# Pooled attention with a gated MLP on one core: batch 0's query loads on ScalarE's queue, w_in's v-half in four loads, the left-over sums apart, and a new opening order

## The chip, the cores and the metric

The kernel runs on one core of a Trainium2 chip. The core has five engines with an instruction stream each: TensorE (PE in the profile), VectorE (DVE), ScalarE (ACT), GpSimd (POOL) and SyncE (SP), which here only issues loads and stores. The metric is device time in microseconds (us), the median over executions; lower is better.

## What is computed

For 8 batches, 8 heads, 576 positions and 64 numbers per head, keys and values are averaged over groups of 8 positions, so 72 of each are left. All 576 queries attend to the 72 pooled keys. The result, 576 x 512 per batch, is the input x of a gated MLP whose output is added to x.

```python
k_p = k.reshape(B, H, Sp, 8, D).mean(axis=3)
v_p = v.reshape(B, H, Sp, 8, D).mean(axis=3)
scores = scale * np.matmul(q, k_p.transpose(0, 1, 3, 2))
attn = np.exp(scores - scores.max(-1)) ; attn = attn / (attn.sum(-1) + 1e-09)
x = np.matmul(attn, v_p)                       # then to (B, S, H*D)
h = gelu_tanh(x @ w_in)                        # 512 -> 1024
u, v = h[..., :512], h[..., 512:]
v_n = (v - mean(v)) / sqrt(var(v) + 1e-06) * g_ln
v_s = einsum('ts,bsd->btd', w_sg, v_n) + b_sg[None, :, None]
out = x + (u * v_s) @ w_out
```

All inputs are float32 but w_in and w_out, which come as float64 and are read as pairs of 32-bit integers.

## The kernel before

The work is cut into steps with a letter, a number and a batch. For a batch: A and B load pooled groups of keys and values (two loads each, per group of four heads), E loads what is left over of the 72 rows after 64 ("left"), C loads the queries of two heads. K sums groups of eight keys; P does so for values. Q turns the queries (into `qT`), S forms the scores of two heads and runs the softmax, T and L turn the probabilities, V multiplies them with the values and writes x, split into two addends (`xhl`) so that the products stay exact. H is the v-half of `x @ w_in` for 128 positions with gelu and normalization, U the u-half, W the product with `w_sg`, O the product with `w_out`, Z the store. A lower-case letter is a weight: `lv0` loads a part of the v-half of w_in, `v0` to `v3` convert and split its quarters, likewise `lu`, `u` for the u-half, `lo`, `o` for w_out, `ls`, `s` for w_sg.

A list, PROLOGUE, gives the order of all these pieces up to the steady state, and PERIOD the order of one batch after that; each mention of a name runs its step up to the next `yield`. Every engine takes its instructions strictly in the order in which they were recorded (the dependencies that the last lines of the function add see to that). So the two lists fix what stands behind what on each engine, and the only freedom at run time is when each waits.

In batch 0, keys and values are summed by TensorE, with a matrix `apart` that picks rows (`pool8`); the left-overs of keys and values lie in one tile, 32 partitions each, and one VectorE instruction sums both (`psum8(lp[64:P], ...)`). ScalarE copies the sums out of PSUM (`kp`), TensorE turns them, ScalarE writes them into `kbd`, and S multiplies `kbd` with `qT`. In later batches VectorE makes the sums.

PSUM is used as two rings of two tiles, `mps` and `aps`; SWAP names the steps that take a tile of the other ring. A tile is taken again only when its last reader is done.

All loads go through SP's queue. A DMA signals one of eight semaphores, taken in turn; a load waits until the one eight before it has landed, so at most eight are under way. The first half of w_in's v-half is one load of 1 MB (`lv0`, 128 x 2 x 1024 integers), the second another (`lv1`). The queries of batch 0 are loaded as they lie in memory (NATURAL), 96 x 6 x 64 numbers for each head: two loads for each of four pairs of heads, the first three pairs into a tile called `early`, the fourth into `qraw`. `early` also holds batch 0's values.

Of the kernel before, what the change touches and what calls it, by code (L numbers as in the profile page):

```python
# [20 lines left out]


PROLOGUE = """
A1+0 A0+0 lv0 E0+0 K0+0 v0 C0+0 C1+0 C2+0 K0+0 C3+0 K1+0 K2+0 K1+0 K2+0 Q0+0 Q1+0 v0 v0 v1 ls0 K2+0 v1 Q0+0 S0+0 Q2+0
Q1+0 S0+0 v1 S1+0 S0+0 B1+0 lv1 S0+0 S1+0 Q2+0 v1 S0+0 S2+0 S1+0 S0+0 S0+0 S2+0 v1 S1+0 v0 S0+0 v0 S2+0 Q3+0 B0+0
Q3+0 S1+0 S3+0 S2+0 S1+0 T0+0 A1+1 S2+0 s3 S1+0 E0+1 S0+0 s4 T0+0 S3+0 S3+0 S3+0 S2+0 S2+0 S1+0 s3 s4 S3+0 s3 S2+0
S3+0 lu0 S3+0 S2+0 s2 s4 P1+0 S3+0 s2 P0+0 v2 A0+1 s2 C0+1 S1+0 S3+0 C1+1 T1+0 v3 L0+0 T2+0 v3 P2+0 L0+0 T1+0 V0+0
lo0 v2 T2+0 V0+0 T3+0 V1+0 v2 v2 s1 v3 K2+1 T3+0 K1+1 K0+1 v3 V1+0 V3+0 v2 V0+0 s1 K2+1 Q0+1 V2+0 s1 v3 B0+1 u0 u0
K2+1 Q1+1 V3+0 V2+0 V1+0 S0+1 S1+1 S0+1 V3+0 u1 V2+0 S0+1 H0+0 H2+0 S1+1 lu1 u0 S0+1 S1+1 V3+0 V2+0 S0+1 S1+1 u1 S0+1
u1 S0+1 H0+0 H0+0 H2+0 C2+1 s0 u1 u0 S1+1 u1 V1+0 H0+0 H3+0 C3+1 s0 V0+0 U1+0 u0 P0+1 S1+1 H2+0 u3 s0 u3 u2 H2+0 u2  # L30
U1+0 H4+0 H0+0 H4+0 Q2+1 T0+1 S1+1 Q3+1 S2+1 T0+1 H2+0 u2 B1+1 S0+1 u3 u2 H4+0 H0+0 H1+0 H2+0 H4+0 T0+1 S2+1 S2+1 u2
H4+0 H3+0 u3 u3 P1+1 H1+0 H3+0 S3+1 S1+1 S3+1 S2+1 S3+1 P2+1 lb0 S2+1 H3+0 U2+0 H1+0 U0+0 o1 S3+1 C0+2 S2+1 U2+0 H4+0
S3+1 H3+0 S3+1 H4+0 S2+1 S3+1 C1+2 A0+2 U3+0 H1+0 U0+0 H3+0 P2+1 S2+1 H4+0 S3+1 K0+2 P2+1 o1 T1+1 H1+0 lo1 A1+2 U3+0
L0+1 P2+1 L0+1 H1+0 L0+1 o0 W2+0 V0+1 o1 L0+1 o0 T1+1 W3+0 T1+1 B0+2 o0 E0+2 o1 o0 V1+1 Q0+2 o1 V0+1 W2+0 K1+2 o3 o3
T2+1 T2+1 o0 T2+1 W3+0 V1+1 W0+0 V2+1 Q1+2 o2 T3+1 o2 T3+1 W0+0 o3 B1+2 W1+0 o2 W3+0 K2+2 T3+1 W1+0 V1+1 K2+2 V2+1
W0+0 V3+1 W3+0 K2+2 S0+2 S1+2 W0+0 C2+2 W2+0 C3+2 W1+0 V3+1 P1+2 W1+0 W2+0 S0+2 O0+0 S1+2 o2 O0+0 Q2+2 S0+2 O1+0 O0+0
o2 V0+1 S1+2 S0+2 o3 o3 P0+2 V2+1 O1+0 A0+3 A1+3 S2+2 V3+1 O2+0 P2+2 S1+2 S2+2 S2+2 V1+1 O1+0 C0+3 O2+0 S0+2 O2+0
H2+1 V3+1 Z0+0 T0+2 Z0+0 H2+1 Q3+2 Z1+0
""".split()
# [776 lines left out]
```

## Time and profile before

| | |
|---|---|
| median of 3 runs | 573.52 us (573.29 to 575.09) |
| the profiled run | 575.11 us, span 573.3 us, granted clock 0.997 |
| TensorE busy | 552.2 us, 96% of the span |
| VectorE | 408.8 us, 71% |
| ScalarE | 345.9 us, 60% |
| GpSimd | 229.8 us, 40% |
| moved by DMA | 46.34 MB |

A busy share over the whole span is a mean over an opening, seven periods of 66 us in which TensorE works without a pause, and an end. In the views, a row of the timeline gives start, length, engine, line, operation, tiles (written<-read), count, and in brackets how long the engine had stood idle ahead of it and what ended that. L166 is the one line from which all loads are issued and L111 the one from which nearly all products are, so there the tiles tell the steps apart: `mps<-xhl,wih` 128x288 is U, `mps<-wih,xhl` 128x512 is H, `aps<-kbd,qT` is S, `ident,e` is T, `ident,el` is L.

### The profile page before, as it was taken

What the parts mean: (1) busy time and instruction counts of PE and PEld (TensorE: products, weight loads), DVE (VectorE), ACT (ScalarE), POOL (GpSimd) and SP (SyncE); (2) the same over time, 40 slices, a digit from 0 to 9 for tenths busy, and PEclk for the clock granted to TensorE, in tenths of its full rate; (3) what the DMA queues carried; (4) which work ended last, traced back from release to release, by engine and by line L of the source; (5) the groups of instructions that cost most, each with busy time, mean ns of one, the idle gap of its engine ahead of it and who ended that gap; (6) DMA issues with size and microseconds to landing.
All of it is one profiled execution on the core that took longest, in us unless ns stands there. A gap on an engine that the chain in (4) does not pass through costs nothing.

```text
span 573.3 us, 10301 instructions
## 1 busy us (share of the span) xinstructions
PE 552.2 (96%) x3793; PEld 520.9 (91%) x3793; DVE 408.8 (71%) x570; ACT 345.9 (60%) x947; POOL 229.8 (40%) x310
## 2 busy tenths in 40 slices
PE   3799999999999999999999999999999999999996
PEld 3677799998999999998999989999999989998996
DVE  1889999888568775878667785778667765344454
ACT  1588695977558755677647766497546775412320
POOL 3477765753144341713325331523416131433240
PEclk9899999999999999999999999999999999999999
DMA  7996545164413435152421625132440211021105
GB/s 196 312 244 164 107 144 116 20 136 78 97 24 74 82 71 105 38 104 62 96 34 44 115 57 106 51 77 46 96 79 1 43 21 22 1 42 22 21 1 84
DMA packets 161602, 46.34 MB, mean 81 GB/s; under 512 B 149072, under 2 KB 149072, under 8 KB 161552
## 3 DMA queue, kind: packets, MB, share of 16 engines
q1 hardware_dynamic: 156688, 45.10, 36.4%
q10 hardware_dynamic: 4864, 0.59, 0.7%
q8 instruction: 30, 0.49, 0.4%
q14 instruction: 20, 0.16, 0.1%
HBM read 36.23 MB, written 9.44 MB: 80 GB/s over the span
## 4 chain that ended last, share of the span: by engine, by line
PE 85%; DMA 5%; DVE 4%; ACT 2%; SPq 2%; issue 1%; POOL 0%; DVEq 0%; ACTq 0%
PE mps L111 68%; PE aps L111 13%; PE aps L146 3%; SPq L166 2%; DMA raw<-in_moe_w_in 2%; DMA kvraw<-in_k 1%; DMA stage<-in_moe_w_sg 1%; DVE kp L335 1%; DMA qraw<-in_q 1%; ACT lt L506 0%; DVE vp L335 0%; DVE lp L335 0%; ACT vl L414 0%; DVE e L485 0%; DVE e L460 0%
## 5 line engine op out<-in xcount | busy, mean ns | idle before, releaser
L111 PE MATMUL mps<-xhl,wih 128*128 128x288 f32 x512 | 89.8, 297 | 0.0
L111 PE MATMUL mps<-wih,xhl 128*128 128x512 f32 x248 | 83.0, 401 | 0.1
L111 PEld LDWEIGHTS mps<-xhl,wih 128*128 128x128 f32 x512 | 75.8, 188 | 1.5
L687 POOL TENSOR_TENSOR glo<-u,ghi 128x576 fp32r<-128x576 f32 x28 | 40.1, 1443 | 91.8 <-ACT ghi L685 91.8
L467 ACT ACTIVATE e<-aps,nmax 128x72 f32<-128x72 f32 x240 | 73.2, 352 | 1.5 <-DVE nmax L450 1.2
L111 PE MATMUL mps<-wsh,vhh 128*128 128x288 f32 x248 | 57.1, 301 | 0.1
L467 ACT ACTIVATION_READ_ACCUMULATOR e<-aps,nmax 128x1 f32 x240 | 57.1, 239 | 0.0
L111 PEld LDWEIGHTS mps<-wih,xhl 128*128 128x128 f32 x248 | 46.6, 188 | 10.6 <-DVE x L726 0.3
L111 PE MATMUL mps<-wsh,vhl 128*128 128x288 f32 x248 | 55.7, 295 | 0.0
L111 PE MATMUL mps<-wsl,vhh 128*128 128x288 f32 x248 | 55.4, 294 | 0.0
L111 PE MATMUL mps<-xhl,wil 128*128 128x288 f32 x256 | 55.0, 296 | 0.0
L111 PE MATMUL mps<-ghi,woh 128*128 128x288 f32 x240 | 54.1, 301 | 0.4 <-DVE u L655 0.4
L557 POOL TENSOR_TENSOR xhl<-x,xhl 128x576 fp32r<-128x576 f32 x32 | 45.3, 1427 | 22.6 <-ACT xhl L555 22.6
L605 DVE TENSOR_SCALAR vg<-vg,mv,rstd 128x512 f32<-128x512 f32 (+1 forms) x40 | 40.3, 1007 | 19.4 <-POOL rstd L603 19.4
L602 POOL TENSOR_TENSOR rstd<-mv,eps 128x1 f32<-128x1 f32 (+1 forms) x40 | 10.7, 267 | 105.3 <-DVE mv L600 95.9
L111 PE MATMUL mps<-glo,woh 128*128 128x288 f32 x240 | 52.7, 295 | 0.0
L111 PE MATMUL mps<-ghi,wol 128*128 128x288 f32 x240 | 52.6, 295 | 0.0
L676 DVE SCALAR_TENSOR_TENSOR mps<-mps,gcol,bbc 128x576 f32<-128x576 f32 x27 | 22.2, 824 | 39.1 <-PE mps L111 39.1
L111 PE MATMUL mps<-wil,xhl 128*128 128x512 f32 x124 | 49.0, 395 | 0.0
L595 ACT ACTIVATE vg<-mps 128x512 f32<-128x512 f32 x31 | 18.5, 598 | 47.4 <-PE mps L111 47.2
L615 POOL TENSOR_TENSOR vhl<-vg,vhh 128x512 fp32r<-128x512 f32 x32 | 41.8, 1308 | 8.5 <-ACT vhh L613 8.5
L111 PE MATMUL aps<-kbd,qT 128*128 128x144 f32 x300 | 41.2, 288 | 2.7 <-DVE e L485 1.4
(208 smaller groups left out, 1427.1 us busy)
## 6 DMA issues: line engine op xcount, KB each, us to landing
kvraw<-in_k SPq DMA_DIRECT2D x32, 256.0 KB
qraw<-in_q SPq DMA_DIRECT2D x112, 72.0 KB
out<-y SPq DMA_DIRECT2D x112, 72.0 KB
kvraw<-in_v SPq DMA_DIRECT2D x28, 256.0 KB
raw<-in_moe_w_in SPq DMA_DIRECT2D x4, 1024.0 KB
raw<-in_moe_w_out SPq DMA_DIRECT2D x2, 1024.0 KB
stage<-in_moe_w_sg SPq DMA_DIRECT2D x4, 288.0 KB
left<-in_k SPq DMA_DIRECT2D x16, 64.0 KB
```

What stands on the lines that cost most here:

```text
L111: nc.tensor.matmul(o, lhsT, rhs, start=start, stop=stop)
L146: nc.tensor.transpose(ps[:rows, i * P:(i + 1) * P], src(i), ident if i < NT - 1 else swap)
L166: queue.dma_start(o, i)
L335: nc.vector.tensor_reduce(out=o, in_=t.rearrange("p a (r d) -> p a d r", r=POOL), axis=AX.X, op=ALU.add)
L467: nc.scalar.activation(e[:, i, h], slots[i][:, h], AF.Exp, bias=nmax[:, i, h:h + 1], **acc)
L557: (nc.vector if b in LO_DVE else nc.gpsimd).tensor_tensor(xhl[:, 1, g], x32[:, g], xhl[:, 0, g].bitcast(F32), op=ALU.subtract)
L595: nc.scalar.activation(vg, o, AF.Gelu_apprx_tanh)
L602: nc.gpsimd.tensor_tensor(rstd, mv[:, 1:2], eps[:n, 1:2], op=ALU.add)
L605: nc.vector.tensor_scalar(vg, vg, mv[:, 0:1], rstd, op0=ALU.subtract, op1=ALU.mult)
L615: (nc.gpsimd if i < NT - 1 else nc.vector).tensor_tensor(lo, vg, hi.bitcast(F32), op=ALU.subtract)
L676: nc.vector.scalar_tensor_tensor(vs, vs, gcol[:, d:d + 1], bbc.rearrange("p (a n) -> p a n", a=2), op0=ALU.mult, op1=ALU.add)
L687: nc.gpsimd.tensor_tensor(glo[:, d], uf, ghi[:, d].bitcast(F32), op=ALU.subtract)
```

## The change

Four edits to the code and new tables:

- `load_q` issues the query loads of batch 0 through ScalarE's queue (`nc.scalar`).
- `load_w` loads the v-half of w_in in four pieces of 512 KB, named lv0 to lv3, two to a tile.
- `load_left` of batch 0 comes in two parts, keys (E0) and values (E1), and the sum of the left-overs in two instructions: keys in K2, values in P2. The memset of `lp` covers 96 partitions.
- PROLOGUE and SWAP are new; PERIOD is as it was.

```diff
-A1+0 A0+0 lv0 E0+0 K0+0 v0 C0+0 C1+0 C2+0 K0+0 C3+0 K1+0 K2+0 K1+0 K2+0 Q0+0 Q1+0 v0 v0 v1 ls0 K2+0 v1 Q0+0 S0+0 Q2+0
+E0+0 A1+0 C1+0 C0+0 lv0 Q1+0 A0+0 Q1+0 Q0+0 C2+0 K2+0 Q0+0 K1+0 lv1 ls0 K0+0 C3+0 v0 K1+0 v0 K0+0 K2+0 v0 K2+0 S0+0
...
-    SWAP = ("H3.0", "K0.0", "K1.0", "K2.1", "L0.1", "Q1.0", "Q2.0", "S1.0", "S3.0", "T0.0", "T0.1", "T1.0", "T2.0", "T2.1", "V1.0", "V2.1", "V3.1", "W0.0", "s4",)
+    SWAP = ("H3.0", "K1.0", "L0.1", "P0.0", "P1.0", "Q0.0", "Q2.0", "S0.0", "S1.0", "S3.0", "T0.0", "T0.1", "T2.0", "T2.1", "T3.0", "U2.1", "V2.0", "V2.1", "V3.0", "W0.0", "s1", "s3", "s4",)
...
-    nc.gpsimd.memset(lp[0:64], 0.0)
+    nc.gpsimd.memset(lp[0:96], 0.0)
...
         if name == "v":
-            sv = sv[:, 2 * j:2 * j + 2, m * lo:m * (lo + NB)]
+            raw = st.get(("w", name, j // 2))
+            if raw is None:
+                raw = st["w", name, j // 2] = per.tile([P, 2, m * NB], I32 if wide else F32, name="raw", tag=tags[j // 2])
+            load(raw[:, j % 2], sv[:, j, m * lo:m * (lo + NB)], nc.gpsimd if name in W_POOL else nc.sync)
+            return
...
-    def load_left(b):
-
-        t = per.tile([P, 2, POOL * D], F32, name="left")
+    def load_left(b, part=None):
+
+        t = st["left", b] if part == 1 else per.tile([P, 2, POOL * D], F32, name="left")
         src = k[b].rearrange("(g h) (j r) d -> h j g (r d)", h=2, r=POOL)
-        for h in range(2):
-            load(t[96:P, h], src[h, JM:SP])
+        if part != 1:
+            for h in range(2):
+                load(t[96:P, h], src[h, JM:SP])
+        st["left", b] = t
+        if part == 0:
+            return
...
-                load(t[:, :, h], q[b, 2 * g + h].rearrange("(t p) d -> p t d", t=6))
+                load(t[:, :, h], q[b, 2 * g + h].rearrange("(t p) d -> p t d", t=6), nc.scalar)
...
     def step_E(b, i):
-        load_left(b)
+        load_left(b, i if b in BY_PE else None)
...
         st["lp", b] = lp
-        psum8(lp[64:P], st["left", b][64:P])
+        r = slice(96 if b in BY_PE else 64, P)
+        psum8(lp[r], st["left", b][r])
...
+        if b in BY_PE:
+            psum8(lp[64:96], st["left", b][64:96])
+            yield
         vp = st.pop(("vp", b))
```

ScalarE at the start of the program. Before, it begins with the conversion of w_in (`top<-raw`), and the copies of the pooled keys (`kp`) stand behind that:

```order
L207 ACT_TABLE_LOAD
L207 ACTIVATE top<-raw 128x512 [waits DMAHW4_49]
L211 ACTIVATE raw<-raw 128x512
L346 COPY kp<-mps 128x128 [waits PE_49] x2
L207 ACTIVATE top<-raw 128x512
L211 ACTIVATE raw<-raw 128x512
```

Now, with what each waits for (DMAHW0 to DMAHW7 are the eight semaphores of loads):

```order
L166 DMA early<-in_q 96x6x64 x3
L166 DMA early<-in_q 96x6x64 [waits DMAHW0_49]
L440 ACT_TABLE_LOAD
L440 COPY qT<-mps 128x576 [waits PE_49]
L166 DMA early<-in_q 96x6x64 [waits DMAHW7_49]
L166 DMA early<-in_q 96x6x64 [waits DMAHW2_49]
L440 COPY qT<-aps 128x576 [waits PE_49]
L166 DMA qraw<-in_q 96x6x64 [waits DMAHW5_49]
L166 DMA qraw<-in_q 96x6x64 [waits DMAHW7_49]
L211 ACTIVATE top<-raw 128x512
L215 ACTIVATE raw<-raw 128x512
L353 COPY kp<-mps 128x128 [waits PE_49]
```

The eight query issues and two copies of turned queries stand ahead of the conversion and of the copies of pooled keys; five of the issues wait for a load that went out earlier.

VectorE in the later part of batch 0's softmax (`nmax` is the negated maximum, `ssum` the sum, `e` the exponentials; the third and fourth reciprocal are in it). Before:

```order
L470 TENSOR_REDUCE ssum<-e 128x10 x2
L482 RECIPROCAL ssum<-ssum 128x10
L450 TENSOR_REDUCE nmax<-aps 128x10
L460 TENSOR_TENSOR e<-aps,nmax 128x720
L482 RECIPROCAL ssum<-ssum 128x10
L470 TENSOR_REDUCE ssum<-e 128x10
L171 TENSOR_TENSOR wsl<-mps,wsh 128x576
L482 RECIPROCAL ssum<-ssum 128x10
L253 TENSOR_TENSOR wtl<-aps,wth 64x576
L171 TENSOR_TENSOR wsl<-mps,wsh 128x576
```

Now:

```order
L481 TENSOR_REDUCE ssum<-e 128x10
L493 RECIPROCAL ssum<-ssum 128x10
L471 TENSOR_TENSOR e<-aps,nmax 128x720
L342 TENSOR_REDUCE lp<-left 32x128
L493 RECIPROCAL ssum<-ssum 128x10
L257 TENSOR_TENSOR wtl<-aps,wth 64x576
L481 TENSOR_REDUCE ssum<-e 128x10
L493 RECIPROCAL ssum<-ssum 128x10
L342 TENSOR_REDUCE kp<-kvraw 128x128
L171 TENSOR_TENSOR wsl<-aps,wsh 128x576
L171 TENSOR_TENSOR wsl<-mps,wsh 128x576
```

The sum of the left-over values (`lp<-left`) and `wtl` stand ahead of the last reciprocal, one `wsl` behind it, and a sum of batch 1's keys (`kp`) directly behind the last reciprocal.

TensorE around the S steps of batch 1 that stand between H steps of batch 0. Before: T, then S, then H (`mps<-wih,xhl`):

```order
L111 MATMUL mps<-wih,xta 128x512
L146 MATMUL mps<-ident,e 128x128 x4
L146 MATMUL mps<-swap,e 128x128
L111 MATMUL aps<-kbd,qT 128x144 x5
L111 MATMUL mps<-wih,xhl 128x512
L111 MATMUL mps<-wil,xhl 128x512
```

Now the H step stands ahead, then S, T, S and U:

```order
L111 MATMUL mps<-wil,xhl 128x512
L111 MATMUL mps<-wih,xhl 128x512 x4
L111 MATMUL aps<-kbd,qT 128x144 x5
L146 MATMUL mps<-ident,e 128x128 x4
L146 MATMUL mps<-swap,e 128x128
L111 MATMUL aps<-kbd,qT 128x144 x5
L111 MATMUL mps<-xhl,wih 128x288 x4
```

The H step that followed the first S is ahead of it, and the second S follows the first with only a T between. In exchange the H step of the last 64 positions (`xta`) has moved to the third place of the H steps.

## Rows read from the trace of the kernel before

**Rows 1.** The page: busy us of each engine with its share of the span and its number of instructions; and, in 40 equal slices of the span (14.33 us each), the GB/s that DMA moved.

```profile
PE 552.2 (96%) x3793; PEld 520.9 (91%) x3793; DVE 408.8 (71%) x570; ACT 345.9 (60%) x947; POOL 229.8 (40%) x310
...
GB/s 196 312 244 164 107 144 116 20 136 78 97 24 74 82 71 105 38 104 62 96 34 44 115 57 106 51 77 46 96 79 1 43 21 22 1 42 22 21 1 84
```

**Rows 2.** Busy time by stretch. Columns: from:to and length in us, then busy us and instructions of PE, weight loads, DVE, ACT and POOL, the granted clock, the DMA engines' share, GB/s. The first rows cut the span at points of the program, the last four are stretches with one kind of load each.

```profile
0.00:7.15 7.15, 0.00 (x0) 0.03 (x1) 1.89 (x2) 1.28 (x1) 5.65 (x22) 1.00 0.58 174
7.15:20.85 13.70, 10.11 (x60) 9.43 (x61) 5.04 (x5) 4.84 (x12) 2.54 (x2) 0.88 0.93 236
20.85:33.76 12.91, 10.24 (x83) 9.11 (x82) 11.60 (x17) 7.63 (x13) 8.10 (x14) 1.00 1.03 338
33.76:50.25 16.49, 15.88 (x93) 12.47 (x93) 15.25 (x16) 16.09 (x31) 12.96 (x14) 1.00 0.73 187
50.25:72.04 21.79, 20.37 (x113) 17.08 (x112) 21.29 (x32) 15.16 (x28) 15.00 (x20) 1.00 0.63 130
...
114.34:573.30 458.96, 454.07 (x3145) 432.43 (x3145) 314.46 (x446) 265.79 (x785) 158.22 (x211) 1.00 0.31 60
...
2.00:4.00 2.00, 0.00 (x0) 0.00 (x0) 1.26 (x1) 0.01 (x1) 1.95 (x7) 1.00 0.88 262
4.00:7.00 3.00, 0.00 (x0) 0.00 (x0) 0.00 (x0) 0.00 (x0) 2.37 (x5) 1.00 0.76 228
14.00:17.00 3.00, 1.07 (x8) 0.88 (x9) 2.59 (x3) 2.05 (x6) 0.00 (x0) 0.98 0.92 202
24.00:28.00 4.00, 2.77 (x22) 2.58 (x23) 3.73 (x6) 2.90 (x6) 3.44 (x4) 1.00 1.03 410
```

**Rows 3.** TensorE's waits in the first 130 us: line that waited <- engine, tile and line that ended it: us in all, times, longest.

```profile
PE mps L111 <- DMA kvraw<-in_k: 7.2, 1, 7.2
PE aps L356 <- ACT kp L346: 2.2, 1, 2.2
PE mps L111 <- ACT qT L429: 1.6, 1, 1.6
...
PE aps L111 <- DVE lt L512: 0.5, 1, 0.5
```

**Rows 4.** The timeline of VectorE: the first left-over sum, the integer steps of w_in, the first maximum of the softmax, a subtraction for w_sg, the key sums of batch 1, and the multiplication, transpose and addition around the S steps of batch 1.

```profile
14.35 1.93 DVE L335 TENSOR_REDUCE lp<-left 64x128 f32<-64x1024 f32 x1 [11.09 <-DMA left<-in_v]
16.31 0.43 DVE L213 TENSOR_SCALAR top<-top 128x512 int32<-128x512 int32 x1
16.77 0.69 DVE L214 SCALAR_TENSOR_TENSOR top<-raw,top 128x512 int32<-128x512 int32 x1
...
20.85 0.91 DVE L450 TENSOR_REDUCE nmax<-mps 128x10 f32<-128x720 f32 x1 [1.36 <-PE mps L111]
...
32.89 0.75 DVE L171 TENSOR_TENSOR wsl<-mps,wsh 128x576 fp32r<-128x576 f32 x1
...
41.24 3.87 DVE L335 TENSOR_REDUCE kp<-kvraw 128x128 f32<-128x1024 f32 x2
...
65.80 0.91 DVE L485 TENSOR_TENSOR e<-e,aps 128x720 f32<-128x720 f32 x1
66.62 0.77 DVE L433 STREAM_TRANSPOSE qT<-qraw 128x576 f32<-128x576 f32 x1
67.31 0.65 DVE L591 TENSOR_TENSOR vg<-mps,vg 64x512 f32<-64x512 f32 x1
```

**Rows 5.** The chain of waits that ended last, in order of time, from its first 120 us: start, length, what.

```profile
3.41 9.75 DMA raw<-in_moe_w_in
...
23.62 7.75 DMA kvraw<-in_k
```

**Rows 6.** The timeline of ScalarE: the conversion of w_in's first quarter, the copies of pooled keys, and the first and last of the four copies into kbd.

```profile
13.18 0.66 ACT L207 ACTIVATE top<-raw 128x512 f32<-128x512 f32 x1 [11.17 <-DMA raw<-in_moe_w_in]
...
14.28 0.41 ACT L346 COPY kp<-mps 128x128 f32<-128x128 f32 x2
...
16.77 0.38 ACT L366 ACTIVATE kbd<-aps 64x256 f32<-64x256 f32 x1 [0.95 <-PE aps L358]
...
17.52 0.18 ACT L367 ACTIVATE kbd<-aps 64x32 f32<-64x32 f32 x1
```

**Rows 7.** The timeline of TensorE: the turn of the left-overs, L, the first product of the first H, T and S of batch 1, the first product of the H behind it, the second S, and the U step.

```profile
16.43 0.30 PE L358 MATMUL aps<-ident,lp 128*128 128x128 f32 x1 [1.35 <-DVE lp L335]
...
36.05 0.63 PE L146 MATMUL aps<-ident,el 128*64 128x128 f32 x4 [0.31 <-POOL el L491]
...
50.25 0.49 PE L111 MATMUL mps<-wih,xhl 128*128 128x512 f32 x1
...
64.63 0.60 PE L146 MATMUL mps<-ident,e 128*128 128x128 f32 x4
...
66.76 1.49 PE L111 MATMUL aps<-kbd,qT 128*128 128x144 f32 x10 [1.42 <-DVE e L485]
68.01 0.50 PE L111 MATMUL mps<-wih,xhl 128*128 128x512 f32 x1
...
70.91 1.39 PE L111 MATMUL aps<-kbd,qT 128*128 128x144 f32 x10
72.04 0.79 PE L111 MATMUL mps<-xhl,wih 128*128 128x288 f32 x4
```

**Rows 8.** The timeline of SP's queue: two query loads issued, start and length.

```profile
14.91 1.06 SPq L166 DMA_DIRECT2D qraw<-in_q  x2
```

More of the change, by code (lines that the diff above doesn't have):

```diff
@@ L23 @@
 PROLOGUE = """
-A1+0 A0+0 lv0 E0+0 K0+0 v0 C0+0 C1+0 C2+0 K0+0 C3+0 K1+0 K2+0 K1+0 K2+0 Q0+0 Q1+0 v0 v0 v1 ls0 K2+0 v1 Q0+0 S0+0 Q2+0
[L25 to L38, printed above, removed]
+E0+0 A1+0 C1+0 C0+0 lv0 Q1+0 A0+0 Q1+0 Q0+0 C2+0 K2+0 Q0+0 K1+0 lv1 ls0 K0+0 C3+0 v0 K1+0 v0 K0+0 K2+0 v0 K2+0 S0+0
@@ new lines @@
+v1 S1+0 v1 v0 S0+0 S0+0 E1+0 Q2+0 Q2+0 S2+0 S1+0 S1+0 S0+0 v0 S0+0 S2+0 S0+0 S0+0 S1+0 S2+0 S1+0 Q3+0 s4 Q3+0 v1 v1
+lv2 B1+0 S2+0 S0+0 S0+0 S1+0 S3+0 B0+0 s4 S3+0 S2+0 S1+0 v1 T0+0 S3+0 P2+0 S3+0 S2+0 S2+0 T0+0 s4 P1+0 A1+1 S1+0 s2
+lv3 S3+0 v2 S1+0 s3 S2+0 s3 S3+0 s2 P0+0 A0+1 S3+0 S2+0 K1+1 E0+1 T1+0 S3+0 s3 lu0 s2 C0+1 S3+0 v2 C1+1 P2+0 T2+0
+T1+0 v3 L0+0 v2 T3+0 v3 L0+0 K0+1 v2 V0+0 lo0 T2+0 v3 v2 K2+1 V0+0 v3 V1+0 s1 V2+0 V1+0 s1 V0+0 V1+0 T3+0 K2+1 u0 s1
+K2+1 v3 Q0+1 u0 V3+0 Q1+1 V3+0 S0+1 V2+0 C2+1 u1 S1+1 S0+1 V1+0 V3+0 S0+1 S1+1 S1+1 u1 S0+1 V2+0 H0+0 S1+1 B0+1 H2+0
@@ new lines @@
+lu1 S1+1 V0+0 u1 V2+0 H0+0 S0+1 u0 V3+0 C3+1 S1+1 S0+1 u1 Q2+1 u1 H4+0 H2+0 s0 H0+0 u0 H4+0 S0+1 H3+0 H2+0 P0+1 s0
+H4+0 u0 u3 H0+0 H2+0 u2 s0 u3 u2 H2+0 B1+1 C0+2 H4+0 Q3+1 H0+0 U1+0 S0+1 S1+1 u2 H1+0 u3 U1+0 H0+0 S2+1 H2+0 u3 u2 u2
+T0+1 H4+0 A0+2 P1+1 H3+0 lo1 u3 S2+1 S2+1 S3+1 P2+1 S3+1 H1+0 T0+1 S3+1 T0+1 S2+1 S1+1 H1+0 S2+1 H4+0 o1 U2+0 S3+1
+H3+0 H1+0 A1+2 S2+1 S3+1 S3+1 U3+0 S2+1 H3+0 U2+0 S3+1 S2+1 U0+0 T1+1 K0+2 H1+0 P2+1 P2+1 H1+0 H3+0 S3+1 U3+0 U0+0
+P2+1 H4+0 L0+1 H4+0 H3+0 C1+2 o1 L0+1 lb0 L0+1 o1 W2+0 V0+1 o0 L0+1 o0 o1 W3+0 W2+0 Q1+2 T2+1 T1+1 o1 T1+1 o3 o3 K1+2
@@ L39 @@
+V1+1 W3+0 o0 V0+1 o0 W0+0 T2+1 E0+2 V1+1 o0 T2+1 V0+1 o3 Q0+2 o2 V2+1 T3+1 o2 B0+2 W0+0 V2+1 o2 T3+1 B1+2 W3+0 K2+2
+W2+0 T3+1 W1+0 W0+0 C2+2 V1+1 W2+0 W0+0 K2+2 V3+1 W1+0 K2+2 P0+2 V3+1 W1+0 S0+2 o3 S0+2 P1+2 C3+2 W3+0 S1+2 W1+0 V2+1
+S0+2 S1+2 P2+2 o3 O1+0 O1+0 Q2+2 O0+0 o2 S0+2 O0+0 O1+0 Q3+2 S2+2 o2 O0+0 O2+0 O2+0 V3+1 Z0+0 S1+2 S2+2 A0+3 S2+2
+H2+1 S0+2 H2+1 A1+3 Z0+0 S1+2 Z1+0 C0+3 V3+1 T0+2 O2+0 V1+1
 """.split()
@@ L284, in load_left @@
             load(t[64:96, gp], src[JM:SP, 4 * gp:4 * gp + 4])
-        st["left", b] = t
     def load_q(b, g):
```

## The prediction

> **What bounds the kernel now.** I read the page's busy shares first [rows 1]: TensorE 96% of the span, VectorE 71%. That average hides several regimes, so I cut the span at points of the program [rows 2]. From 114.34 us to the end TensorE is busy 454.07 of 458.96 us: that part is bound by TensorE, and the change leaves its order alone. Before 7.15 us TensorE does nothing, from 7.15 to 20.85 it is busy 10.11 of 13.70 us, and from 20.85 on VectorE is the fuller one at first: 11.60 of 12.91, 15.25 of 16.49, 21.29 of 21.79 us. So the opening has three limits one after the other: data, then VectorE, then both. What can be won is TensorE's idle time before about 72 us; 14.0 of it lies before 50.25 us (7.15 + 3.59 + 2.67 + 0.61, [rows 2]). Then I asked at each step which wait ends last. TensorE waits 7.2 us for the first keys, 2.2 for the pooled keys that ScalarE copies and 1.6 for a copy of turned queries [rows 3]. VectorE's sum of left-over keys and values starts at 14.35 us, when the last left-over values land [rows 4]. ScalarE starts its conversions at 13.18 us, when w_in's first half has landed, a load issued at 3.41 us [rows 5, 6].
>
> I follow one marker: the U step that TensorE begins at 72.04 us [rows 7]. Behind it the same work stands on a full TensorE, so what this start gains or loses, the run gains or loses. The profiled run took 575.11 us for a span of 573.3, so 1.8 us lie around it; the median of the runs is 573.52. I put the difference on the median.
>
> **1. The loads: when ScalarE gets free.** The eight query loads (96 x 6 x 64 numbers, 144 KB each) leave SP's queue. Two issues cost 1.06 us [rows 8], so SP is freed of some 4 us and ScalarE pays them. Only three go out at once. Loads take eight semaphores in turn, whichever queue issues them, and each waits until the load eight before it has landed. By the order of the built program ScalarE's fourth waits for its own first, the fifth for w_in's first quarter, the sixth for the second half of the other keys, the seventh for the second block of w_sg, the eighth for the fifth. Behind these waits stand, on ScalarE, w_in's conversion and the two copies of pooled keys without which no score is formed. The latest of them is the second block of w_sg, so I sum what is ahead of it: 128 KB of left-over keys, 1024 KB of keys, 1024 KB of w_in = 2.23 MB at 410 GB/s; 576 KB of w_sg = 0.59 MB at 338; six query loads = 0.88 MB at 202: the rates of stretches that carried such loads with the engines full [rows 2]. That is 5.4 + 1.8 + 4.4 = 11.6 us. Transfers begin at about 2.3 us (share 0.88 in 2 to 4 us, [rows 2]), so 13.9 us is the early end. The late end: the first slice of 14.33 us moved 196 GB/s = 2.81 MB, and the other 0.89 MB at the next slice's 312 [rows 1] make 17.1 us. I take 14.4, nearer to the early end: w_in's 1 MB, landed at 13.15 [rows 5], held up the issues behind it and now comes in pieces of half the size; the share of 0.76 in 4 to 7 us [rows 2] is the half us that I add.
>
> The Trainium skill speaks against a gain here: "DMA: Bandwidth & Descriptors", section "Issuing engines are not separate DMA queues", says that all issuers feed the same DMA engines and that a second one only saves issue time. The trace agrees as far as it goes: SP's queue alone holds them at a share of 1.03 [rows 2]. Were it otherwise, the 4.4 us of the queries would drop out of the sum.
>
> **2. From that landing to the first softmax step.** Two query issues 1.06 [rows 8]; conversions and copies 1.51 (13.18 to 14.69, [rows 6]); turning keys and left-overs on TensorE some 0.7, of which the left-overs' 0.30 [rows 7]; four copies into kbd 0.93 (16.77 to 17.70) and one more conversion 0.6 [rows 6]; then VectorE's two integer steps for w_in's second quarter, 0.46 + 0.69, which stand ahead of the softmax [rows 4]. Sum 5.95: the first maximum at 20.35 us, with bounds 19.85 and 23.05; before, 20.85. That the left-over sum waits for keys alone, and no longer until 14.35, wins nothing beyond this: ScalarE is late next.
>
> **3. The softmax on VectorE.** The left-over sum becomes two instructions. Over fewer partitions each has as many elements per partition as before, so I price the second as the whole one, 1.93 us [rows 4], and it stands inside the softmax, ahead of the third reciprocal. From the first maximum to the last reciprocal it was 12.91 us (20.85 to 33.76), 1.31 of it idle [rows 2]. Now 1.93 more, one subtraction for w_sg in and one out, and some 0.65 of the idle gone: 14.2 us. The last reciprocal ends at 34.55, 0.8 later. Behind it VectorE now has a key sum (half of 3.87) and a subtraction (0.75, [rows 4]) that frees the bank that L needs: L starts at 37.25, before at 36.05 [rows 7]. One T step (0.7, 64.63 to 65.34, [rows 7]) has gone ahead of L. The rest up to H is the same work: H at 50.25 + 1.2 - 0.7 = 50.7 us.
>
> **4. The H phase.** TensorE stood 1.42 us ahead of the S step at 66.76 [rows 7], until VectorE's multiplication of 65.80 had ended [rows 4]. Now an H step of 2.90 us (68.01 to 70.91, [rows 7]) goes ahead of T and S: TensorE arrives at 50.7 + 14.38 + 2.90 = 68.0. VectorE needed 45.86 us from the first maximum to the end of that multiplication; now 1.93 more, 1.42 more for a transpose (0.77) and an addition (0.65) moved ahead of it [rows 4], and I let 1.4 of its 3.0 us of idle [rows 2] vanish: 20.35 + 45.86 + 3.35 - 1.4 = 68.2. The wait shrinks to 0.2. Then S 1.25, T 0.7, S 1.13 [rows 7] and 0.3 for a Gelu that the second S now waits for (between nothing and 0.9): U at 71.6, 0.5 earlier. w_in's loads in four, the memset of lp over 96 partitions and the changed banks I price at nothing: the loads and the memset lie under ScalarE's waits of step 1, the banks change no duration. Without that cover each costs under 0.6 us (an issue, [rows 8]), and none can gain more than that.
>
> Sum: 573.5 - 0.5 = **573.0 us**. With all of VectorE's idle kept it is 574.5, with none and the early landing 571.8: the likeliest's own range.
>
> **Rivals.** *Slower: ScalarE is held by its own query loads.* Place: ScalarE's seventh and eighth query issue. If the transfers share the engines so that the second block of w_sg lands at 17.1 us, the first maximum is at 23.05, the multiplication ends at 70.9 and U starts at 74.3: 2.3 later, 575.8 us. It decides from a landing of about 16.4 us on. For it: SP alone needed until 13.15 us for w_in's 1 MB [rows 5]. Against: no 1 MB load stands ahead any more. The Trainium skill, "DMA: Bandwidth & Descriptors", section "Queues, rings and completion order", says that an engine goes round its queues packet by packet. No run so far has two load queues to show it; by it a small query load waits through the larger pieces of keys and weights, which would bring this case.
> *Faster: VectorE's idle goes.* Landing at 13.9 and no idle inside the softmax: L at 36.1, H at 49.6, TensorE arrives at S at 66.9 and U starts at 70.0: 2.0 earlier, 571.5; without the wait of 0.5 for lt [rows 3] 571.0. For it: the next keys, held until 31.37 us in the chain [rows 5], and the values ahead of them come earlier, so there is work to fill with. Against: the sum of 1.93 lies in the middle of it.
> *Much faster: the queries cost the keys nothing.* Landing at 9.5 us; TensorE's pooling then sets the copies at about 12, the first maximum comes at about 15.9, and all behind it 4.5 earlier: 568.5. Against it: the full engines of rows 2.
> *It does not do what it says:* the loads don't run ahead of ScalarE's work, as five of eight wait. That is in the forecast.
>
> **How the numbers follow.** A measurement of this kernel tells 0.3% (1.7 us) from no change: under 571.8 is faster, over 575.2 slower. Forecast 0.47; held ScalarE 0.25; idle gone 0.22; free queries 0.06. The forecast's bounds stay inside the 0.3%, so faster is 0.28, same 0.47, slower 0.25. The range takes in the held ScalarE with 0.6 us for one more late load, and the faster case down to 570.0: 570.0 to 576.4.
>
> **What would show it.** The last copy into kbd ends near 18.6 us (held 21.3, free 14); the first maximum 20.4; the last reciprocal ahead of L 34.6; L 37.2; H 50.7; no wait over 0.5 ahead of the first S behind H; U 71.6. I am wrong if the copies of pooled keys start before 14 us, if VectorE stands idle over 2 us between the first maximum and L, or if the difference arises behind the U step.

## The result and the profile after

The changed kernel takes 579.86 us (579.67 to 580.07, 4 runs) against 573.43 us for the kernel before in the same series: ratio 1.0095, 95% interval 1.0074 to 1.0115. It is slower, by 6.4 us, and lies 3.5 us above the upper end of the forecast's range. Its profiled run took 579.67 us for a span of 577.9.

The views are read in the same order as before the change. The page's busy times, which answer to [rows 1], tell nothing: TensorE has the same work and waits longer.

```profile
PE 553.5 (96%) x3793; PEld 522.5 (90%) x3793; DVE 408.4 (71%) x571; ACT 346.4 (60%) x947; POOL 228.5 (40%) x310
```

Cut at the same points of the program as [rows 2] (first product, first maximum, end of the last reciprocal, L, H, U), the loss arises ahead of the first maximum. That stretch, which now begins with the turning of queries at 4.89 us and no longer with the pooling of keys at 7.15, has grown from 13.70 to 20.84 us, with 10.98 us of TensorE's work in it (10.11 before):

```profile
4.89:25.73 20.84, 10.98 (x59) 10.10 (x60) 4.12 (x5) 5.48 (x13) 3.85 (x6) 0.87 1.06 297
25.73:40.07 14.34, 11.33 (x82) 9.87 (x82) 13.53 (x19) 8.15 (x13) 8.53 (x16) 0.95 0.24 88
...
56.05:77.19 21.14, 20.77 (x114) 16.98 (x112) 20.73 (x31) 16.16 (x31) 15.29 (x19) 1.00 0.76 204
```

Then TensorE's waits, the longest first, which answer to [rows 3]:

```profile
PE aps L364 <- ACT kp L353: 5.0, 1, 5.0
PE mps L437 <- DMA early<-in_q: 4.9, 1, 4.9
PE aps L437 <- DMA early<-in_q: 3.8, 1, 3.8
...
PE aps L111 <- DVE lt L523: 0.5, 1, 0.5
```

TensorE now waits first for queries, 4.9 and 3.8 us, and no longer for keys (7.2 us in [rows 3]); the wait for ScalarE's copies of the pooled keys has grown from 2.2 to 5.0 us. So the timeline of ScalarE comes next; ACTq is its queue of DMA issues. It answers to [rows 6]:

```profile
0.72 2.83 ACTq L166 DMA_DIRECT2D early<-in_q  x4
...
10.87 1.67 ACTq L166 DMA_DIRECT2D early<-in_q  x2
12.58 0.64 ACT L440 COPY qT<-aps 128x576 f32<-128x576 f32 x1 [5.82 <-DMA kvraw<-in_k]
15.17 4.18 ACTq L166 DMA_DIRECT2D qraw<-in_q  x2
19.40 0.66 ACT L211 ACTIVATE top<-raw 128x512 f32<-128x512 f32 x1 [6.19 <-DMA early<-in_q]
...
20.68 0.27 ACT L353 COPY kp<-aps 128x128 f32<-128x128 f32 x1
...
22.69 0.18 ACT L375 ACTIVATE kbd<-aps 64x32 f32<-64x32 f32 x1
```

The pair of issues that begins at 15.17 us lasts 4.18 us, where the pair at 10.87 takes 1.67 and the pair of [rows 8] took 1.06: the seventh goes out at 15.2, the eighth stands until 19.0. The chain of waits that ended last (start, length, what) names what it stood for; it answers to [rows 5]:

```profile
3.73 7.12 DMA raw<-in_moe_w_in
...
10.87 8.15 DMA early<-in_q
...
19.04 0.32 ACTq L166
```

ScalarE's fifth query load, issued at 10.87 us when w_in's first quarter had landed, needs 8.15 us for 144 KB, and the eighth issue waits for it. The conversion that stood at 13.18 us before starts at 19.40. TensorE in turn:

```profile
14.02 1.95 PE L111 MATMUL aps<-kvraw,apart 128*128 128x128 f32 x16
21.00 0.69 PE L364 MATMUL aps<-ident,kp 128*128 128x128 f32 x2 [5.04 <-ACT kp L353]
...
22.93 4.83 PE L111 MATMUL aps<-kbd,qT 128*128 128x144 f32 x20 [1.02 <-ACT kbd L375]
...
43.09 0.60 PE L146 MATMUL aps<-ident,el 128*64 128x128 f32 x4
...
56.05 0.49 PE L111 MATMUL mps<-wih,xhl 128*128 128x512 f32 x1
...
73.54 1.39 PE L111 MATMUL aps<-kbd,qT 128*128 128x144 f32 x10
...
75.84 1.49 PE L111 MATMUL aps<-kbd,qT 128*128 128x144 f32 x10 [0.36 <-ACT vg L606]
77.19 0.79 PE L111 MATMUL mps<-xhl,wih 128*128 128x288 f32 x4
```

L, H and U stand 7.0, 5.8 and 5.2 us later than in [rows 7] (whose run took 1.6 us more than its kernel's median); the wait of 1.42 us ahead of the S step behind H is gone. The first S step is 20 passes in 4.83 us. The windows around it show why (columns as in [rows 2]; the clock is the third number from the end):

```profile
18.00:20.00 2.00, 0.00 (x0) 0.00 (x0) 0.00 (x0) 0.60 (x2) 0.00 (x0) 1.00 1.14 202
20.00:22.00 2.00, 0.90 (x3) 0.50 (x3) 1.12 (x2) 1.01 (x5) 0.61 (x1) 0.61 1.03 368
...
24.00:26.00 2.00, 2.00 (x11) 2.00 (x10) 0.98 (x3) 0.63 (x2) 1.26 (x1) 0.50 1.04 374
26.00:28.00 2.00, 2.00 (x14) 2.00 (x14) 1.75 (x3) 0.00 (x0) 0.00 (x0) 0.68 1.03 399
```

Ahead of the products at 21.00 us TensorE was idle for 5.04 us. From 22 to 26 us the granted clock is 0.50 of 2.4 GHz, which is the lower level of 1.2 GHz, and it comes back only in 26 to 28 us. VectorE, which answers to [rows 4]:

```profile
25.73 0.91 DVE L461 TENSOR_REDUCE nmax<-aps 128x10 f32<-128x720 f32 x1 [0.98 <-PE aps L111]
...
35.92 1.94 DVE L342 TENSOR_REDUCE lp<-left 32x128 f32<-32x1024 f32 x1
...
39.85 0.22 DVE L493 RECIPROCAL ssum<-ssum 128x10 f32<-128x10 f32 x1 [0.33 <-POOL ssum L483]
```

From the first maximum to the end of the last reciprocal it is 14.34 us, forecast 14.2. The delay is there before the first maximum: 25.73, against 20.85 before and 20.35 forecast.

One more view is new. SP's queue (SPq) stands from 25.84 to 37.89 us, because the tile of left-overs is free only when VectorE has read its second part (35.92 + 1.94):

```profile
24.65 1.19 SPq L166 DMA_DIRECT2D kvraw<-in_k  x2
37.89 1.49 SPq L166 DMA_DIRECT2D left<-in_k  x2
```

So there are four suspects: (a) ScalarE held by its own late query issues; (b) the low clock behind TensorE's idle time; (c) SP's stand; (d) the second left-over sum inside the softmax. (e) is a rival to (a): the data is late whoever issues the loads, since the DMA engines are full (a share of 1.06 up to the first maximum).

### The profile page after: what moved, and what is told of

It is laid out like the page before. It is cut to its first block, busy times and chain, and to the rows that moved or that the text cites. A ratio compares the mean times of both kernels' runs of the same rounds, so it can differ in the third digit from the quotient of the medians.

```text
span 577.9 us, 10307 instructions
## 1 busy us (share of the span) xinstructions
PE 553.5 (96%) x3793; PEld 522.5 (90%) x3793; DVE 408.4 (71%) x571; ACT 346.4 (60%) x947; POOL 228.5 (40%) x310
## 4 chain that ended last, share of the span: by engine, by line
PE 84%; DVE 6%; DMA 4%; POOL 2%; issue 1%; ACT 1%; SPq 1%; ACTq 0%; POOLq 0%; DVEq 0%
PE mps L111 66%; PE aps L111 14%; PE aps L146 3%; DMA early<-in_q 1%; DMA raw<-in_moe_w_in 1%; SPq L166 1%; POOL top L220 1%; DVE kp L342 1%; DVE lp L342 1%; DVE e L471 1%; DMA kvraw<-in_v 1%; DVE al L540 0%; DVE nmax L461 0%; DMA qraw<-in_q 0%; PE aps L364 0%
## 5 line engine op out<-in xcount | busy, mean ns | idle before, releaser
L111 PE MATMUL mps<-xhl,wih 128*128 128x288 f32 x496 | 87.1, 298 | 0.0
L111 PEld LDWEIGHTS mps<-xhl,wih 128*128 128x128 f32 x496 | 73.3, 188 | 1.6 <-DVE vg L602 0.3
L111 PE MATMUL mps<-xhl,wil 128*128 128x288 f32 x248 | 53.3, 296 | 0.0
L613 POOL TENSOR_TENSOR rstd<-mv,eps 128x1 f32<-128x1 f32 (+1 forms) x40 | 10.8, 269 | 107.5 <-DVE mv L611 97.5
L606 ACT ACTIVATE vg<-mps 128x512 f32<-128x512 f32 x31 | 18.6, 599 | 45.7 <-PE mps L111 45.5
L111 PE MATMUL aps<-kbd,qT 128*128 128x144 f32 x310 | 44.3, 297 | 1.5 <-ACT kbd L375 1.0
```

The costliest lines, as they stand in the source:

```text
L111: nc.tensor.matmul(o, lhsT, rhs, start=start, stop=stop)
L606: nc.scalar.activation(vg, o, AF.Gelu_apprx_tanh)
L613: nc.gpsimd.tensor_tensor(rstd, mv[:, 1:2], eps[:n, 1:2], op=ALU.add)
```

## The experiments

"Before" is measured again beside each; its median was 573.95, 574.07, 574.4 and 574.47 us in the four series. The line that all of the first group edit is the one in `load_q`:

```diff
-                load(t[:, :, h], q[b, 2 * g + h].rearrange("(t p) d -> p t d", t=6), nc.scalar)
+                load(t[:, :, h], q[b, 2 * g + h].rearrange("(t p) d -> p t d", t=6), nc.scalar if g < 2 else nc.sync)
```

**1. The last four query loads on SyncE** (the diff above).

> The changed kernel with the last four of batch 0's eight query loads (C2, C3) issued by SyncE, the first four by ScalarE as before. Theory 'held' (ScalarE stands at its own late query issues, the last one until 19.0 us): w_in's conversion starts near 13 us in place of 19.4, the copies of pooled keys run as soon as TensorE's pooling ends at about 16 us, the first maximum comes near 20.5 us in place of 25.7, and the time falls by 4 to 5 us to about 575. Rival 'transfers' (the DMA engines are full, so the data comes late whoever issues it): SyncE stands at the same two waits, w_sg and the values come later, the first maximum stays above 23.5 us and the time above 578. Rival 'left' (what is lost is SyncE's stand until 37.9 us at the tile of left-overs): the first maximum moves but the time stays at 579 to 580.

573.49 us, ratio 0.9992 (0.997 to 1.0014). The conversion starts at 11.99 us, the first maximum at 19.68. The loss is gone whole, as "held" said; "transfers" falls, and so does "left": SP stands here too, until 31.19 us.

**2. All eight on SyncE** (`nc.scalar` replaced by `nc.sync`).

> The changed kernel with all eight query loads of batch 0 issued by SyncE again: the other parts of the change and the new order are kept. Theory 'held': as with the last four alone or a little better, since ScalarE issues nothing: about 574 to 575.5; the last copy into kbd ends below 19 us. Rival 'transfers': over 578. If ScalarE's queue is of use for the first queries (four issues earlier), this kernel is up to 1.5 us slower than the one with the last four moved.

574.64 us, ratio 1.0014 (0.9995 to 1.0034). In the profiled run of 576.01 us the last copy into kbd ends at 19.29 us, a little above the 19 that I expected, and the first maximum is at 21.09. What is left of the change without the queue (w_in in four loads, the sums apart, the new order) makes no difference that can be measured. ScalarE's first four issues may be worth a microsecond (experiment 1 is 1.15 us lower), as the expectation's last sentence has it; the intervals overlap.

**3. Only the last two on SyncE** (`nc.scalar if g < 3 else nc.sync`).

> The changed kernel with only the last two query loads (C3: ScalarE's seventh and eighth issue) given to SyncE. Theory 'held', narrow form (the eighth issue alone, which waits for the fifth load to land at 19.0 us): as much is won as with four loads moved, first maximum near 20.5 us, about 575. Wide form (the fifth and sixth issues hold ScalarE too, until 12.6 us): 1 to 2 us less is won, 576 to 577. Rival 'transfers': over 578.

573.43 us, ratio 0.9983 (0.9961 to 1.0004): the narrow form holds, moving the seventh and eighth issue is enough. Who waits for the fifth load now is seen on SP's queue:

```profile
13.42 1.08 SPq L166 DMA_DIRECT2D qraw<-in_q  x2
15.00 2.07 SPq L166 DMA_DIRECT2D left<-in_v  x2
18.83 0.35 SPq L166 DMA_DIRECT2D raw<-in_moe_w_in  x1
```

and on ScalarE:

```profile
10.77 1.67 ACTq L166 DMA_DIRECT2D early<-in_q  x2
12.48 0.64 ACT L440 COPY qT<-aps 128x576 f32<-128x576 f32 x1 [5.73 <-DMA kvraw<-in_k]
13.02 0.66 ACT L211 ACTIVATE top<-raw 128x512 f32<-128x512 f32 x1
```

The fifth load is again issued at 10.8 us. In the built program the load that waits for its semaphore is now w_in's third quarter, on SP, and it goes out at 18.83, as the eighth query load did at 19.0. The load lands as late as before (18.81 against 19.02); the wait for it has moved to an engine that has nothing else to do. First maximum 20.02, U at 70.78.

**4. TensorE kept busy** while ScalarE stands.

```diff
...
+                for _ in range(18 if i == 0 else 0):
+                    mm(full[:, 1, 0:P], apart, ident, True, True)
...
```

The 18 products write to the unused half of the tile `full`, which the pooling takes.

> The changed kernel with 18 products of 128 x 128 added on TensorE between the pooling of the keys and their turning, where it stands idle from 16.0 to 21.0 us; their output goes to an unused half of a PSUM tile. Nothing else is changed. Theory 'clock' (part of the loss is the low granted clock of 22 to 26 us, which follows that idle time): the 20 passes of the first S step take near 2.7 us in place of 4.83, the first maximum comes near 23.6 us, and the time falls by about 2 us to 577.8. If the low clock has nothing to do with the idle time, or VectorE makes up for it, the time stays at 579.9 within 0.5.

578.62 us, ratio 1.0081 (1.0055 to 1.0107), 1.24 us below the changed kernel, where I expected about 2. The two ratios' intervals overlap, so the times alone do not show a gain. The row that decides:

```profile
23.25 2.72 PE L111 MATMUL aps<-kbd,qT 128*128 128x144 f32 x20 [1.02 <-ACT kbd L378]
```

2.72 in place of 4.83 us: without the idle time the S step runs at the higher clock. First maximum 24.99, U 75.78, 1.41 earlier than in the one profile of the changed kernel. The added products ended late, so the second copy of pooled keys waited 0.61 us for them; without that the clock's share would be up to 2.0 us, by my estimate.

**5. The kernel before once more.**

> The kernel before, unchanged, for a second profile of it: the first one came from its longest run (575.11 us). If the spread between runs lies in the opening (the arrival of loads), U starts about 1 to 1.5 us ahead of 72.04 in a run near the median and the stretch from U to the end is 501.3 us again; if it lies behind U, U starts at 72.0 and that stretch is shorter by what the run is shorter.

573.69 us (8 runs). The profiled run took 574.95 us, the most of the eight, with U at 71.80 and 573.2 - 71.80 = 501.4 us behind it: too near to the first profile to decide for this kernel. The new order answers it instead. From U to the end of the span it is 577.9 - 77.19 = 500.71 in the changed kernel, 571.5 - 70.78 = 500.72 in experiment 3, and 500.70 to 500.84 in the nine other profiles of that order, whose runs took 571.42 to 579.16 us. All of their spread lies ahead of U.

**6. The queue alone, in the kernel before** (its `load` of the queries given `nc.scalar`).

> The kernel before with one part of the change alone: batch 0's query loads issued by ScalarE, at their old place in the order (behind w_in's first conversion, two of them between the two copies of pooled keys). Theory 'held': ScalarE now stands at the issues' waits ahead of the copies of pooled keys, the last of them for a load eight before; the first maximum comes 3 to 6 us later than 20.85 and the time is 576 to 579.5. Rival: the queue is harmless and the loss needs the new order or the four w_in loads: 573 to 574.5.

582.65 us, ratio 1.014 (1.0108 to 1.0171): 8.6 us lost, some 3 us more than the most that I expected. The loss needs neither the new order nor the four loads of w_in.

```profile
12.82 6.75 ACTq L166 DMA_DIRECT2D early<-in_q  x4
19.62 0.27 ACT L346 COPY kp<-mps 128x128 f32<-128x128 f32 x1 [6.82 <-DMA early<-in_q]
20.43 1.72 ACTq L166 DMA_DIRECT2D qraw<-in_q  x2
22.20 0.27 ACT L346 COPY kp<-mps 128x128 f32<-128x128 f32 x1 [2.31 <-DMA early<-in_v]
```

Both copies of pooled keys (14.28 in [rows 6]) stand behind issues, the second behind one that waits for a load of values. The first maximum comes at 27.94.

**7. All eight on ScalarE, the last two behind the copies into kbd.**

```diff
-E0+0 A1+0 C1+0 C0+0 lv0 Q1+0 A0+0 Q1+0 Q0+0 C2+0 K2+0 Q0+0 K1+0 lv1 ls0 K0+0 C3+0 v0 K1+0 v0 K0+0 K2+0 v0 K2+0 S0+0
+E0+0 A1+0 C1+0 C0+0 lv0 Q1+0 A0+0 Q1+0 Q0+0 C2+0 K2+0 Q0+0 K1+0 lv1 ls0 K0+0 v0 K1+0 v0 K0+0 K2+0 v0 K2+0 C3+0 S0+0
```

> The changed kernel with all eight query loads still on ScalarE, but its last two issues (C3) placed behind the four copies into kbd instead of ahead of w_in's conversion. The loads and their semaphores are the same. Theory 'held by place' (what counts is what stands behind the waiting issue): conversions start at about 13 us, the last copy into kbd ends near 18 us, the first maximum comes near 20 to 21 us, plus at most 1 us when the issues wait until 19 us ahead of the next conversion; the time is 573 to 575. Rival 'the queue' (two load queues at once are the trouble, wherever the issues stand): above 577.

579.56 us: my expectation failed by 4.6 us, though its first half came true. The time is the one that the rival "the queue" named (above 577), but experiments 1, 3 and 9 use two load queues as well and lose nothing that can be measured, so two queues as such are not the trouble. On ScalarE

```profile
16.85 0.18 ACT L375 ACTIVATE kbd<-aps 64x32 f32<-64x32 f32 x1
19.26 1.10 ACTq L166 DMA_DIRECT2D qraw<-in_q  x2
20.41 0.66 ACT L211 ACTIVATE top<-raw 128x512 f32<-128x512 f32 x1 [3.38 <-DMA early<-in_q]
```

the copies end at 17.0 us and the first S step starts at 17.08. But the next conversion stands behind the issue, VectorE's integer steps behind that, and the first maximum behind them, at 22.18. And the queries issued so late are missed themselves: the second of the two loads lands at 27.41 us by its semaphore's records, TensorE turns the fourth pair at 27.66 us after 2.71 us of idle time, and VectorE stands 3.53 us for the fourth maximum, at 32.68. So the waiting issue cost about the same at both places on ScalarE, the second time by another way; what removed the cost was another engine (experiments 1 and 3) or a wait that ended early (experiment 9).

**8. The second left-over sum early** (experiment 3, with `E1+0` ahead of `ls0` and the first `P2+0` behind the second `K2+0`).

> The changed kernel with C3 on SyncE, and in addition the left-over values loaded ahead of w_sg and their sum (1.96 us on VectorE) placed ahead of the second pair of integer steps, where VectorE stands idle (14.9 to 18.9 us), instead of inside the softmax. Theory 'VectorE bounds the stretch from the first maximum to L': the first maximum stays near 20.0 to 20.5 us, the last reciprocal comes at about 32 us in place of 33.5, L, H and U 1.5 to 2 us earlier than with C3 on SyncE alone (36.7, 49.7, 70.8), and the time is 571.5 to 572. SyncE's stand at the tile of left-overs ends as well, since that is read by about 17 us. Rival 'another wait takes its place' (ScalarE's weights, GpSimd's multiplications or the next keys): 573 to 573.6, and the trace names it.

573.65 us, ratio 0.9984 (0.9968 to 1.0001), against 571.5 to 572 expected: no gain over experiment 3. The profiled run took 571.92 us, the least of twelve. The stretch from first maximum to the end of the last reciprocal shrinks only from 13.67 to 12.86 us, since VectorE then stands 1.29 us for GpSimd's `ssum`. So the sum inside the softmax, suspect (d), is worth 0.8 us of that stretch at most, and none in the median. SP's queue is free earlier here as well, with no gain either.

**9. C2 on SyncE, C3 on ScalarE** (`nc.sync if g == 2 else nc.scalar`).

> The changed kernel with the fifth and sixth query load (C2) on SyncE and the last two (C3) still on ScalarE. Now ScalarE's last two issues wait for w_in's first quarter and for a key load, which landed at 10.4 and about 11.2 us in earlier runs, and no longer for a load of ScalarE's own queue. Theory 'slow neighbour' (the loss comes from the one wait for ScalarE's fifth load, which its queue brings slowly beside SyncE's): ScalarE is free by about 13 us, the first maximum near 20 to 21 us, the time 573 to 574.5, with six loads on ScalarE's queue as good as with six in the other choice. Rival 'late issues as such' (any issue behind the first four holds ScalarE for long): above 576.

574.72 us, ratio 1.0008 (0.9991 to 1.0024). The rival (above 576) falls, ScalarE's conversion starts at 12.11 and the first maximum in the profiled run is at 18.09 us. But that run took 571.42 us and the nine others 573.56 to 576.13, so the profile does not show what makes the median 0.2 us higher than I allowed; it stays open. Whether ScalarE's queue is a slow one, as "slow neighbour" has it, is taken up with the rivals below.

**10 to 12. Towards a faster head.** With `g < 2` on ScalarE, the keys are loaded first, pooled ahead of the second pair of queries, and copied ahead of w_in's conversion:

```diff
-E0+0 A1+0 C1+0 C0+0 lv0 Q1+0 A0+0 Q1+0 Q0+0 C2+0 K2+0 Q0+0 K1+0 lv1 ls0 K0+0 C3+0 v0 K1+0 v0 K0+0 K2+0 v0 K2+0 S0+0
...
+A1+0 A0+0 C1+0 C0+0 E0+0 lv0 Q1+0 Q1+0 C2+0 K1+0 K0+0 K2+0 Q0+0 lv1 ls0 C3+0 K1+0 K0+0 v0 Q0+0 K2+0 v0 v0 K2+0 S0+0 v1
...
```

Behind the `v1` the list goes on as it was.

> C2 and C3 on SyncE, and a new head of the order: the keys of batch 0 are loaded first (ahead of the left-over keys and of w_in's first quarter), TensorE pools them ahead of turning the second pair of queries, and ScalarE copies the pooled keys ahead of w_in's first conversion. Keys' four loads, issued by 3.3 us, should land by about 7 to 8 us in place of 11.2 us. Theory 'the way to the first S step bounds the opening': pooling runs from about 7 to 12 us, the last copy into kbd ends near 15 us, and the first maximum comes 1 to 3 us earlier than 20 us; if VectorE and the H phase keep their lengths, the time is 570.5 to 572.5. Rival 'the next wait' (w_in's second quarter, whose integer steps stand ahead of the first maximum on VectorE, or the later queries): the first maximum stays at 19.5 to 20.5 us and the time at 573 to 574.

571.4 us, ratio 0.9952 (0.9935 to 0.9969). Pooling starts at 6.23 us (10.90 in the changed kernel), the first maximum is at 16.50, and the next wait is the fourth pair of queries:

```profile
21.15 0.69 PE L437 MATMUL aps<-ident,qraw 96*128 96x96 f32 x6 [0.92 <-DMA qraw<-in_q]
```

Only a part of the 3.5 us that the first maximum is ahead of experiment 3 reaches U (69.48 against 70.78).

> As the kernel with the keys first, but the second quarter of w_in is loaded ahead of the queries C2 on SyncE. If w_in's second quarter (conversion on ScalarE behind the copies into kbd, integer steps on VectorE ahead of the first maximum) is what the keys-first kernel waits for, this one has the first maximum up to 1.5 us earlier; if the queries C2 are late instead (TensorE's third turning), it is 0.5 to 1 us slower than the other. Time 570.5 to 573.5.

573.0 us, ratio 0.9978 (0.9956 to 0.9999; `lv1 C2+0` in place of `C2+0 ... lv1`). Its median is 1.6 us above the other's, as expected in direction if queries are late, though the intervals just overlap. The late ones are not the third pair, C2, but the fourth: in its profiled run (576.32 us, the most of twelve) TensorE waits 3.12 us for them, and the first maximum, 17.12, is no earlier. So w_in's second quarter was not the limit.

> The kernel with the keys first, with one thing moved: SyncE issues the last query loads (C3) ahead of w_sg's five loads instead of behind them. In the keys-first run TensorE stood 0.92 us for these queries at 21.15 us and VectorE 0.62 us behind it, and ScalarE 0.94 us. If their lateness is what is left, the fourth maximum comes about 0.6 to 1 us earlier (24.09 before) and the time is 570.4 to 571.2; if w_sg's last block, turned right behind them, is then late instead, the time stays at 571.4 within 0.4.

570.9 us, ratio 0.9938 (0.9917 to 0.9959; `lv1 C3+0 ls0` in place of `lv1 ls0 C3+0`). The time is inside the range expected, but not by the way expected: TensorE no longer waits for those queries, yet the fourth maximum comes at 25.14 us and not ahead of 24.09. ScalarE stood 1.11 us for w_in ahead of the conversion at 12.59 and 1.10 us ahead of the one at 16.27, and the clock took some back: behind 2.22 us of idle time the first S step needs 4.39 us.

```profile
15.22 4.39 PE L111 MATMUL aps<-kbd,qT 128*128 128x144 f32 x20 [2.22 <-ACT kbd L375]
```

This kernel beats both: 3.6 us below the kernel before in its series, 9 us below the changed one. Against experiment 10 it is no clear gain, for the intervals overlap.

## Why the prediction was wrong

**Step 1 failed, at one sentence**: "The latest of them is the second block of w_sg, so I sum what is ahead of it." The sum came near: that block let the seventh issue go at 15.2 us, inside the bounds of 13.9 and 17.1. In part that is luck, for of the six query loads that it counts ahead of the block the fifth and sixth landed behind it, at 19.0 and 19.9. But the list just ahead of it had the eighth issue waiting for the fifth load, and the step took that wait to end earlier, so that it had no term for it. It ended 3.9 us later, at 19.04. The fifth load is issued only at 10.87, when w_in's first quarter has landed, and needed 8.15 us. Conversions started at 19.40 instead of 14.4 + 1.06 = 15.46: 3.9 us. Experiments 1, 3 and 9 show that this wait, on ScalarE, is the cause; experiment 3 shows that the same load, as late and waited for by SP, costs nothing. In the changed kernel the load was hardly slower than SP's: by the last record of each load's semaphore, the five loads of w_sg that SP issued from 6.94 to 11.55 us needed 7.1 to 8.0 us each, and SP brought two query loads of the same size in 7.2 and 6.6 us in experiment 1 (C2) and in 8.4 and 8.8 in experiment 10 (C3). It landed late because it was issued late.

**Step 2** forecast 4.9 us from the first conversion to the first maximum; it took 6.3. Most of the missing 1.4 us is the clock, a term that the sum did not have: in experiment 4 the stretch takes 5.7 us, of which 0.6 is the wait for the added products. ScalarE's delay left TensorE idle for 5.04 us, and the forecast, for its rival too, did not ask at which clock TensorE would come back. [Rows 2] held a hint, 0.88 for the stretch around the same wait of 2.2 us.

**Step 3**: the softmax took 14.34 us, forecast 14.2. Some of it is the low clock too, for in experiments 3 and 4 it was 13.67 and 13.68. L came 3.0 us behind the last reciprocal, forecast 2.7, and H 12.96 us behind L, forecast 13.45.

**Step 4** came true: no wait ahead of the S step behind H, 0.36 us for a Gelu ahead of the second S (forecast 0.3), and U 21.14 us behind H, forecast 20.9.

In experiment 3, where ScalarE is free in time, the whole chain of the forecast can be read: last copy into kbd 18.2 (forecast 18.6), first maximum 20.02 (20.4), end of the last reciprocal 33.7 (34.6), L 36.72 (37.2), H 49.69 (50.7), U 70.78 (71.6), time 573.43 (573.0). So the marks hold within 1.0 us. For the first two that is partly luck, since the way there is another one:

```profile
10.52 1.22 PE L437 MATMUL aps<-ident,early 96*128 96x96 f32 x6 [4.44 <-DMA early<-in_q]
...
14.39 1.95 PE L111 MATMUL aps<-kvraw,apart 128*128 128x128 f32 x16
...
16.38 0.27 ACT L353 COPY kp<-aps 128x128 f32<-128x128 f32 x1 [1.52 <-PE aps L111]
```

ScalarE begins its conversions at 13.02 us, 2.4 ahead of the forecast's 15.46, and then stands 1.52 us until TensorE's pooling of the keys has ended. TensorE in turn had waited 4.44 us for the second pair of queries, which the new order turns ahead of the pooling; before, the pooling began at 7.15 us. The forecast's sum has no term for this (only its *much faster* rival counts the pooling), and it is what experiment 10 takes away.

**The account of the 6.4 us.** U in the changed kernel is 6.41 us later than in experiment 3, which is as fast as the kernel before. Of this 5.71 arise ahead of the first maximum and 0.67 inside the softmax. Experiment 4 gives 1.4 to 2.0 to the clock, from one trace each; the other 4.4 to 5.0 us, what is left of the sum, are ScalarE standing. The rows agree: in the changed kernel the pooling ends at 14.02 + 1.95 = 15.97 us and its second copy starts at 20.68, 4.7 us later, where in experiment 3 it follows at once. SP's stand and the second sum, suspects (c) and (d), cost nothing that could be measured.

**The rivals.** *Held ScalarE* named the right place, "ScalarE's seventh and eighth query issue", at a price of 2.3 us instead of 6.4: its condition was the landing of the block of w_sg, and the clock was missing. Its sign, a last copy into kbd at 21.3 us, was passed too: 22.87. The rule of the Trainium skill that stood beside it ("DMA: Bandwidth & Descriptors", section "Queues, rings and completion order": an engine goes round its queues packet by packet) is neither borne out nor ruled out by this trace. The queues between 10.8 and 19.0 us (q1 is SP's, q10 ScalarE's):

```profile
q1 hardware_dynamic: 925, 2.04, 79.6%
q10 hardware_dynamic: 1716, 0.43, 33.2%
```

ScalarE's queue moved 0.43 of 2.47 MB in packets of some 250 bytes, SP's 2.04 MB in packets of some 2,200. But SP's loads of w_sg took nearly as long as ScalarE's load, as said. Only in experiment 9 do ScalarE's late loads, 10.2 and 8.7 us, stand clearly behind SP's of w_sg, 6.7 to 7.6. I gave this case 0.25 because no large load stood ahead; a small load issued late was enough. *Idle gone* and *free queries* did not come. *It does not do what it says* was half true: the fifth to eighth load were issued at 10.9 to 19.0 us, not ahead of ScalarE's work.

## What to carry to other kernels

A DMA issue on an engine that computes is an instruction that can wait, and everything behind it on that engine waits too (here 3.9 us at the eighth issue). List each issue's own wait, and price each of them by when the load that it waits for is itself issued, plus the time that loads then need (here 7 to 8 us), not by the order of issue. A delay that leaves TensorE idle can be paid a second time at the lower clock (here 1.4 to 2.0 us). To start loads early, give the second queue only as many as go out nearly without a wait, and put first the data on which the longest chain hangs (experiments 10 and 12).

## What was not expected of the hardware

The lower clock was not there at once: in the window of 18 to 20 us TensorE is idle at a granted 1.00. The fall comes just before work resumes at 21.00 (cut finer, 1.00 from 20.00 to 20.25 us, 0.91 to 20.50, 0.50 from there), and 0.50 holds through a full stretch of products until 26 us. The length of the last wait alone does not tell: behind 1.93 us (experiment 10) the S step took 2.72 us, behind 2.22 us (experiment 12) 4.39. In experiment 12 TensorE had stood 0.74 us more just before, with one product of 0.30 us in between.

A load of 144 KB took 8.15 us from issue to landing, and 8.04 in experiment 3 (10.77 to 18.81). In the kernel before, by the records of its semaphores, query loads of the same size issued from 13.2 to 15.5 us needed 3.6 to 4.4 us, and those issued from 7.9 to 9.1 us 6.9 to 7.0.
